# Batch 3 by quadrant attention, with copies and exponentials dealt anew, in a dilated attention and squared-ReLU FFN kernel

## The chip, the cores and the metric

The kernel runs on one core of one Trainium2 chip. The metric is the device time of an execution in microseconds, of which the median of several executions is given. Beside it stands one execution that the hardware profiler recorded; its span runs from the first to the last instruction.

Engines are named as the profile names them: PE (TensorE, matrix products; PEld its weight loads), DVE (VectorE), ACT (ScalarE), POOL (GpSimd, which here issues loads), SP (SyncE, which here issues stores and transposes).

## The reference

Eight batches of eight heads, 576 tokens, head dimension 64. Heads 0 to 3 attend to the last 32 tokens, heads 4 to 7 to every fourth of the last 128. The output of attention, 4608 tokens of 512, goes through a feed-forward net (FFN) with a squared ReLU.

```python
def _attn_ref(q, k, v):                      # (8, 8, 576, 64)
    window, dilation = 32, 4
    scores = 1.0 / np.sqrt(D) * np.matmul(q, k.transpose(0, 1, 3, 2))
    rel = pos[:, None] - pos[None, :]
    mask_plain = (rel >= 0) & (rel < window)
    mask_dil = (rel >= 0) & (rel < window * dilation) & (rel % dilation == 0)
    # heads 0-3 plain, heads 4-7 dilated; softmax over the unmasked scores
    return np.matmul(attn, v)

def _moe_ref(x, w_in, w_out):                # (4608, 512), (512, 2048), (2048, 512)
    h = np.maximum(x @ w_in, 0.0)
    return h * h @ w_out
```

## The kernel before

**FFN.** Tokens go through the FFN in tiles of 512, the first 1024 in tiles of 256. A tile is cut into groups, numbered over the whole kernel: groups 0 to 31 are the first 512 tokens, 32 to 63 the second, and from 64 on each tile of 512 has 32 groups. Of these the first 16 make one unit each of the first product (four matmuls of 512 columns over the four row blocks of `xT`, line 880), which ACT takes from PSUM with a ReLU (893) and DVE squares in place (894) into `h2T`. The last 16 are the second product (922): four token blocks `m`, each in four parts, and part `x` reads units 4x to 4x + 3. ACT copies each finished block to `osb` (928) and SP stores it. PSUM has four buffers `pf` for all this.

In a tile that is `early` (the first two of 512 that begin at token 512 or 1024) the first four units are begun on three row blocks of `xT` (order 0, 2, 1, 3) in two groups of six matmuls and closed with the fourth in two groups of two. A row block of `xT` is one pair of heads, `e` = 0 to 3.

**Attention** is woven into the groups. Pairs of heads come in the order e = 0, 2, 1, 3; e = 0, 1 are plain heads, 2, 3 dilated. There are two forms of it.

Batches 1 to 3 go through `step`. `kbd` and `vbd` hold block-diagonal matrices of two heads, so that matmuls are 128 x 128: `scores` (codes a, b) with an exponential on ACT and a mask multiplication on DVE, `pv` (codes o, p) with the weighted sum, the sum of weights, Ln and Exp on ACT (the reciprocal) and a multiplication into `xT`. Batch 2's dilated pairs and all of batch 3 take q and k from a transposing DMA (`cross`, into `xx`) and copy them into `qT` and `kbd` by `halves` (codes q, k), batch 1 transposes on PE. Batch 3 (`ADDED`) also adds overlapping pieces of the weights on DVE (`pm`), so that the sum of weights needs fewer matmul columns.

Batches 4 to 7 (`NATURAL`) go through `natural_step`. Their matmuls work on 64 x 64 quadrants of the array (line 529 in `quadrants`), four side by side, and v stays in rows (`load_v_rows`). Codes: K, Q, R are the copies of one batch into `k_both` (in `kbd`), `q_both` (in `qT`) and `last` (in `kbd`), all on DVE (499, 496, 504 and 507); each K code is two instructions, each Q code one, each R code two. S is the scores of a pair; B is the weighted sum of the pair before and then the scores of this pair, called a bundle here; E the exponential of one half of the scores and its mask (656, 658); L the four Ln (637, 638); X the Exp (642) and three multiplications into `xT` (645, 647). In the text L0 is the L of pair e = 0, E10 and E11 the two halves of pair 1.

**The order** is written out by hand. `PROGRAM` has a field for each group with the codes that follow it, and a list `steps` of group numbers and codes for the quadrant batches is merged behind it. Each engine takes its instructions in that order. For batch b the first bundle stands at group 32(b - 1) - 4, the others 8 groups apart, E at 2 and 3 groups after the bundle, L with the next bundle and X one group after. The copies stand in pairs of codes at 12, 10, 8, 6 and 3 groups ahead of the first bundle, the second code of each one group later. A tile needs all the batches that it overlaps: tile 96 to 127 (tokens 1536 to 2047) needs all of batch 3, tile 128 to 159 batch 4.

Buffers that decide about waits: `kbd` and `qT` are single, so copies for a batch wait until the batch before has read them; `xx` and `vbd` are double by batch; scores have two `pa` buffers, both used by every bundle; `po` and `pd` are single.

Of the kernel before, what the change touches and what calls it, by code (L numbers as in the profile page):

```python
# [12 lines left out]
RES = 4  # L13

ORDER = (0, 2, 1, 3)
# [13 lines left out]
    "| 2k0 1V2 | 1b2 1p0 | 1b1 1V3 1K3 | | 1p2 1p1f | 2a0 1b3 | 2k1l 2b0 2o0 1p3f 2k1h | 2q1 2k2 L3:x | | 2q2 2p0 "  # L29
    "L3:vwpdr 2a1 | | | 2b1 | 2o1 2a2 2v2 2q3 | | 2p1f | 2k3 | 2b2 2o2 | 2v3 | 2a3 2p2f L4:q10123 | 2b3 2o3 | 3k1 "  # L30
    "| 2p3 | 3q1v L4:q00123 | 3k0l | | 3a1 3k0h | | 3k2l | 3o1 3q0a | 3k2h | | | 3a0 | 3b1 | 3q2 | | 3p1 L4:x "
    "L4:V | 3v2 | 3b0 | 3a2 3q3l 3o0 3q3h 3k3 | | | 3o2 3b2 | | 3p0 3v3 | 3a3 | 3p2 | L5:q10123 3b3 | 3o3 | | | "
    "L5:q00123 3p3 L5:V | | | | | | | | | | | | L5:x | | | | L6:q00123 | | | | | | | | | | | | | L6:q10123"
)
# [27 lines left out]
def kernel(  # L62
# [9 lines left out]
    nc = tc.nc  # L72
    P = nc.NUM_PARTITIONS
    B, H, S, D = q.shape
# [3 lines left out]
    bf16 = mybir.dt.bfloat16  # L78
# [3 lines left out]
    ALU = mybir.AluOpType  # L82
# [12 lines left out]
    STAGE = (0, 1, 0, 2, 2, 2, 2, 2)  # L95
    ADDED = 3
    NATURAL = 4
    RING = 4 * S
# [5 lines left out]
    p_pool = ctx.enter_context(tc.tile_pool(name="p", bufs=4))  # L104
    pm_pool = ctx.enter_context(tc.tile_pool(name="pm", bufs=4))
    r_pool = ctx.enter_context(tc.tile_pool(name="r", bufs=2))
# [119 lines left out]
    def trans(b: int, e: int, nm: str, part: int, home: str):  # L226

        pool, name = (ps_f, "pf") if "f" in home else (ps_a, "pa")
        ps = pool.tile([P, 1024], bf16, name=name)
        t = staged(b, nm)  # L230
        copy = copier(nm, e, home, True)
        if b == 2:
            m0, n, pitch, cuts = 0, M, M, [(t[0:80, a, :, :], MS[a], 80) for a in range(2)]
        else:

            m0, n, pitch, cuts = MS[part], MN[part], 80, [(t[0:80, part, :, :], 0, 80)]
        pv_ = ps[:, 0 : 4 * pitch].rearrange("p (h c m) -> p h c m", h=2, c=2)
        for hl in range(2):
            for c in range(2):
                for src, c0, w in cuts:  # L240
                    nc.tensor.transpose(  # L241
                        pv_[:, hl, c, c0 : c0 + w], src[:, 2 * e + hl, P * c : P * c + P], ident[0:w, 0:w]
                    )
        ready[b, e, nm] = pv_[:, :, :, 0:n], m0, n, copy
        halves(e, nm, *ready[b, e, nm], (0,) if "l" in home else (0, 1))

    ready = {}

    def copier(nm: str, e: int, home: str, early: bool):
        act = "a" in home or "v" not in home and nm == "q" and e < NE // 2 and early  # L250
        return nc.scalar.copy if act else nc.vector.tensor_copy
# [31 lines left out]
    def blocks(b: int, e: int, part: int):  # L283
# [3 lines left out]
        if e < NE // 2:  # L287
            if b >= ADDED:
                return [(i, None, 16 * i, min(16 * i + 24, M)) for i in (range(4, NB) if part else range(4))]
            if part == 0:  # L290
                return [(i, None, 16 * i, min(16 * i + 24, 64)) for i in range(4)]
            return [(3, None, 64, 72)] + [(i, None, 16 * i, min(16 * i + 24, M)) for i in range(4, NB)]
# [7 lines left out]
    def half_at(b: int, e: int):  # L300

        if e < NE // 2:
            return (384, mask_p[:, 384:832]) if b >= ADDED else (352, mask_p)
        return (256, mask_d) if b in PARTED else (416, mask_h)

    pts, pms = {}, {}

    def scores(b: int, e: int, part: int):
# [5 lines left out]
        for i, r, m0, m1 in blocks(b, e, part):  # L314
# [14 lines left out]
            out=pt[:, off : off + n], in0=pt[:, off : off + n],  # L329
            in1=mask[:, off : off + n] if b < ADDED and mask is not mask_h else mask[:, 0:n], op=ALU.mult,  # L330
        )
        if b < ADDED:
            return
        pm = pms[e, part] = pm_pool.tile([P, 160], bf16, name="pm")

        def add(to, x, y):
            nc.vector.tensor_tensor(out=to, in0=x, in1=y, op=ALU.add)

        if e >= NE // 2:
            main = pt[:, off : off + 352].rearrange("p (r c) -> p r c", r=2)  # L340
            add(pm[:, 0:64].rearrange("p (r m) -> p r m", r=2), main[:, :, 64:96], main[:, :, 96:128])
            return
        i0, n = (3, 4) if part else (0, 3)
        v = pt[:, 96 * i0 : 96 * (i0 + n + 1)].rearrange("p (i r m) -> p i r m", r=RES, m=24)
        add(
            pm[:, 0 : 32 * n].rearrange("p (i r m) -> p i r m", r=RES, m=8),
            v[:, 0:n, :, 16:24], v[:, 1 : n + 1, :, 0:8],
        )
        if part:
            add(  # L350
                pm[:, 128:160].rearrange("p (r m) -> p r m", r=RES), v[:, n, :, 16:24],
                pt[:, 768:832].rearrange("p (r m) -> p r m", r=RES)[:, :, 0:8],
            )

    def pv(b: int, e: int, part: int, spare=None, name=""):
# [11 lines left out]
        if byr:  # L367
# [8 lines left out]
            mms.append((o3[:, :, 128:M], 8, rem))  # L376
            if b >= ADDED:
                pm = pms[e, part][:, 0:64].rearrange("p (r m) -> p r m", r=2)
                dms += [(d3[:, :, 0:64], main[:, :, 0:64]), (d3[:, :, 64:96], pm), (d3[:, :, 96:M], main[:, :, 128:176])]
            else:  # L380
                dms += [(d3[:, :, 0:96], main[:, :, 0:96]), (d3[:, :, 64:M], main[:, :, 96:176])]
            dms.append((d3[:, :, 128:M], rem))
        else:
            n = RES * MN[part]
            o3 = o[:, 0:n].rearrange("p (r m) -> p r m", r=RES)
            d3 = d[:, 0:n].rearrange("p (r m) -> p r m", r=RES)
            if not dil and b >= ADDED:

                i0 = 4 * part
                p4 = pt[:, 96 * i0 : 96 * i0 + 384].rearrange("p (i r m) -> p r i m", r=RES, m=24)  # L390
                d4 = d3.rearrange("p r (i m) -> p r i m", m=16)
                pm = pms[e, part]
                if part == 0:
                    dms.append((d4[:, :, 1:4, 8:16], p4[:, :, 1:4, 8:16]))
                    dms.append((d4[:, :, 1:4, 0:8], pm[:, 0:96].rearrange("p (i r m) -> p r i m", r=RES, m=8)))
                    dms.append((d4[:, :, 0, :], p4[:, :, 0, 0:16]))
                else:
                    dms.append((d4[:, :, 0:4, 8:16], p4[:, :, :, 8:16]))
                    b3 = pt[:, 288:384].rearrange("p (r m) -> p r m", r=RES)
                    b8 = pt[:, 768:832].rearrange("p (r m) -> p r m", r=RES)  # L400
                    dms.append((d4[:, :, :, 0:8], pm[:, 0:160].rearrange("p (i r m) -> p r i m", r=RES, m=8)))
                    dms.append((d4[:, :, 4, 8:16], b8[:, :, 8:16]))
                    mms.append((o3[:, :, 0:8], 3, b3[:, :, 16:24]))
                    mms.append((o3[:, :, 64:80], 8, b8))
                for i in range(4):
                    m1 = min(16 * i + 24, 64) if part == 0 else 16 * i + 24
                    mms.append((o3[:, :, 16 * i : m1], i0 + i, p4[:, :, i, 0 : m1 - 16 * i]))
            elif dil and part == 0:
                dms.append((d[:, 0:n], pt[:, 0:n]))
# [36 lines left out]
    def step(b: int, code: str):  # L446
# [6 lines left out]
        if what in "qk" and (b > XB or b == XB and e >= NE // 2):  # L453
            t = (qx if what == "q" else kx)[b % 2]
            halves(e, what, t[:, 2 * e : 2 * e + 2, :, :], 0, M, copier(what, e, home, b < ADDED), his)
        elif what in "qQkK" and "h" in home:
# [395 lines left out]
    def ffn_groups(tk0: int, nt: int):  # L852

        early = NT <= tk0 <= 2 * NT
        h2 = h2_pool.tile([P, NF, NT], bf16, name="h2T")
# [197 lines left out]
    groups[NF:G] = [head[y] for y in (8, 9, 12, 13, 10, 11, 14, 15)] + head[24:32]  # L1055
    COPIES = ("K00 K01", "K10 K11", "Q00 Q01", "Q10 Q11", "R00 R01")
    START = {NATURAL: (-10, -9, -3, -2, -1)}
    for b in range(NATURAL, B):
        base = G * (b - 1) - 4
        for y, codes in zip(START.get(b, (-12, -10, -8, -6, -3)), COPIES):  # L1060
            steps += [(base + y + x, b, code) for x, code in enumerate(codes.split())]
        for x, e in enumerate(ORDER):
            at = base + 8 * x
            steps.append((at, b, f"{'S' if b == NATURAL and x == 0 else 'B'}{e}"))
            steps += [(at + 2, b, f"E{e}0"), (at + 3, b, f"E{e}1"), (at + 8, b, f"L{e}"), (at + 9, b, f"X{e}")]
    steps.append((G * (B - 1) - 4, B - 1, f"P{ORDER[-1]}"))
    steps.sort(key=lambda x: (x[0], x[2][0] in "LX"))
    program = [x.split() for x in PROGRAM.split("|")]
    for code in program[0]:
        run(code)  # L1070
    for g, group in enumerate(groups):
# [10 lines left out]
        while steps and steps[0][0] <= g:  # L1082
            natural_step(*steps.pop(0)[1:])

# [29 lines left out]
```

## Time and profile before

| | us |
|---|---|
| median of 3 executions | 311.77 (309.77, 311.77, 312.34) |
| profiled execution | 308.71 |
| its span | 306.8 |
| PE busy | 295.2 (96%) |
| ACT busy | 203.4 (66%) |
| DVE busy | 177.7 (58%) |
| POOL busy | 96.1 (31%) |
| groups 64 to 95 on PE, start to start | 87.83 to 123.39 |
| groups 96 to 127 | 123.39 to 154.42 |
| groups 128 to 159 | 154.42 to 185.66 |
| groups 160 to 191 | 185.66 to 216.90 |

The busy times are shares of the whole span; stages differ much in them. The last four rows are read from the timeline of PE, from the first matmul of a tile's first product to that of the next tile. The granted clock of TensorE is 1.00 in every stretch.

### The profile page before, as it was taken

The page shows a single profiled execution, that of the slowest core. Times are in us where ns is not written, and L with a number is a line of the kernel's source. Part 1 is how long each engine was busy: PE and PEld are TensorE (multiplying, and loading weights), DVE is VectorE, ACT ScalarE, POOL GpSimd, SP SyncE. Part 2 cuts the span into 40 slices and gives each one's busy share as a digit, 9 for nine tenths or more (in the row PEclk, how much of TensorE's full clock was granted, in tenths as well). Part 3 has the DMA queues.
Part 4 walks back from the last instruction along what each step waited for, and adds up shares of the span by engine and source line. Part 5 has one row for each costly group of instructions (what it writes and reads, how often), then busy time and mean ns, then how long its engine had stood idle before and what let it go on. Part 6 is the DMA issues. An engine that isn't in the chain of part 4 may idle for free.

```text
span 306.8 us, 7297 instructions
## 1 busy us (share of the span) xinstructions
PE 295.2 (96%) x2870; PEld 172.3 (56%) x2903; DVE 177.7 (58%) x517; ACT 203.4 (66%) x439; POOL 96.1 (31%) x138
## 2 busy tenths in 40 slices
PE   8899999999999978999999999999999999999995
PEld 3599658769655544554455445544554445445543
DVE  1675567988988995468456855676563234104400
ACT  6888478869869744786579657865786576226511
POOL 8599683893065056230161208000000000000000
PEclk9999999999999999999999999999999999999999
DMA  8999999999979969998299869902200210121022
GB/s 115 196 180 214 204 162 224 174 150 185 154 111 196 157 100 204 139 148 131 69 133 152 103 142 103 164 16 65 61 2 13 68 61 0 35 71 34 0 64 75
DMA packets 80290, 35.09 MB, mean 114 GB/s; under 512 B 49920, under 2 KB 75648, under 8 KB 80256
## 3 DMA queue, kind: packets, MB, share of 16 engines
q0 software_dynamic: 46592, 18.23, 52.6%
q1 hardware_dynamic: 32976, 16.06, 26.0%
q8 instruction: 23, 0.38, 0.5%
q10 hardware_dynamic: 688, 0.33, 0.5%
q14 instruction: 11, 0.09, 0.1%
HBM read 36.90 MB, written 9.44 MB: 151 GB/s over the span
## 4 chain that ended last, share of the span: by engine, by line
PE 86%; DVE 6%; ACT 4%; issue 2%; ACTq 0%
PE pf L922 37%; PE pf L880 36%; PE po L674 2%; PE pa L529 2%; ACT h2T L893 2%; PE pd L529 1%; PE pa L241 1%; DVE h2T L894 1%; PE po L529 1%; PE po L427 1%; PE pa L704 1%; PE pd L429 1%; DVE kbd L499 1%; PE pf L756 1%; PE pa L323 1%
## 5 line engine op out<-in xcount | busy, mean ns | idle before, releaser
L880 PE MATMUL pf<-xT,w_in 128*128 128x512 bf16 (+1 forms) x693 | 130.4, 340 | 0.8
L922 PE MATMUL pf<-w_out_sb,h2T 128*128 128x512 bf16 (+2 forms) x570 | 128.6, 373 | 2.1 <-issue 1.4
L880 PEld LDWEIGHTS <-w_in 128*128 128x128 bf16 x704 | 76.9, 114 | 44.6 <-issue 1.1
L893 ACT ACTIVATE h2T<-pf 128x512 bf16<-128x512 f32 x144 | 82.4, 605 | 17.5 <-PE pf L880 17.0
L894 DVE TENSOR_TENSOR h2T<-h2T 128x512 bf16<-128x512 bf16 x144 | 60.1, 425 | 57.3 <-ACT h2T L893 53.0
L922 PEld LDWEIGHTS <-h2T 128*128 128x128 bf16 x592 | 54.7, 98 | 58.6
L928 ACT COPY osb<-pf 128x512 f32<-128x512 f32 (+1 forms) x36 | 20.7, 576 | 40.5 <-PE pf L922 37.6
L166 POOL DMA_DIRECT2D qb<-in_q_dram x18 | 13.6, 757 | 44.0 <-DMA xx<-qb 32.4
L645 DVE TENSOR_TENSOR xT<-po,rec 128x512 bf16<-128x512 f32 x16 | 11.1, 692 | 23.3 <-ACT rec L642 22.1
L656 ACT ACTIVATE pt<-pa 128x448 bf16<-128x448 f32 (+3 forms) x32 | 16.3, 509 | 9.3 <-DVE xT L647 9.3
L475 POOL DMA_DIRECT2D vd<-in_v_dram x16 | 9.9, 634 | 28.3 <-PE pa L529 24.8
L638 ACT ACTIVATE rec<-pd 64x512 f32<-64x512 f32 x32 | 18.6, 580 | 0.0
L183 POOL DMA_DIRECT2D vbd<-in_v_dram x20 | 13.9, 708 | 8.3 <-DMA kb<-in_k_dram 2.3
L327 ACT ACTIVATE pt<-pa 128x352 bf16<-128x352 f32 (+6 forms) x24 | 11.9, 506 | 4.1 <-PE pa L317 2.9
L431 ACT ACTIVATE rec<-pd 128x256 f32<-128x256 f32 (+2 forms) x19 | 7.8, 410 | 10.1 <-PE pd L429 10.1
L166 POOL DMA_DIRECT2D kb<-in_k_dram x18 | 13.6, 758 | 0.8 <-DMA vbd<-in_v_dram 0.4
L637 ACT ACTIVATE rec<-pa 64x64 f32<-64x64 f32 x32 | 7.0, 219 | 10.1 <-PE pa L529 9.5
L499 DVE COPY kbd<-xx 64x320 bf16<-64x320 bf16 (+1 forms) x32 | 13.0, 508 | 0.4
L484 POOL DMA_DIRECT2D vbd<-in_v_dram x16 | 12.5, 798 | 0.4 <-DMA qb<-in_q_dram 0.4
L442 DVE TENSOR_TENSOR xT<-po,rec 128x256 bf16<-128x256 f32 (+2 forms) x19 | 8.6, 454 | 6.5 <-ACT rec L432 5.7
L432 ACT ACTIVATE rec<-rec 128x256 f32<-128x256 f32 (+2 forms) x24 | 10.6, 443 | 0.8
L642 ACT ACTIVATE rec<-rec 128x576 f32<-128x576 f32 x16 | 10.9, 680 | 0.3
(128 smaller groups left out, 308.2 us busy)
## 6 DMA issues: line engine op xcount, KB each, us to landing
qb<-in_q_dram POOLq DMA_DIRECT2D x7, 320.0 KB, 5.4
kb<-in_k_dram POOLq DMA_DIRECT2D x7, 320.0 KB, 7.0
vd<-in_v_dram POOLq DMA_DIRECT2D x32, 64.0 KB, 6.2
w_in<-in_moe_w_in_dram POOLq DMA_DIRECT2D x4, 512.0 KB, 7.1
w_out_sb<-in_moe_w_out_dram POOLq DMA_DIRECT2D x4, 512.0 KB, 12.8
out_dram<-osb SPq DMA_DIRECT2D x16, 128.0 KB, 4.1
qb<-in_q_dram POOLq DMA_DIRECT2D x7, 256.0 KB, 7.2
kb<-in_k_dram POOLq DMA_DIRECT2D x7, 256.0 KB, 8.2
```

What stands on the lines that cost most here:

```text
L166: nc.gpsimd.dma_start(t[0:n, part, hs, :], src[b, hs, t0 : t0 + RES * n, :].rearrange("h (p r) d -> p h (r d)", r=RES))
L183: nc.gpsimd.dma_start(dst[rows, e, i0:i1, rows], v[b, 2 * e + hl, 64 * i0 : 64 * i1, :].rearrange("(i p) d -> p i d", p=64),)
L484: nc.gpsimd.dma_start(v_rows[b % 2][rows, e, :, :], v[b, 2 * e + hl, :, :].rearrange("(i p) d -> p i d", p=64))
L499: nc.vector.tensor_copy(k_both[rows, :, :].rearrange("p h (i m c j) -> p j c h i m", c=2, j=2, m=16)[:, jj, c, :, g::2, :], kx[b % 2][src, ...
L529: nc.tensor.matmul(out[sides[c]], lhs, rhs, start=begin, stop=True, skip_group_check=True)
L638: nc.scalar.activation(rec[to, 0:512], d[at, :], ACT.Ln)
L656: nc.scalar.activation(pt, sp[b, e][g][:, 0:n], ACT.Exp, scale=SCALE)
L880: nc.tensor.matmul(to, w_in_sb[piece][:, kt, c0 : c0 + 509 : 4], rhs, start=(kt == kts[0] and x == 0), stop=(kt == kts[-1] and x == per - ...
L893: nc.scalar.activation(hv, acc[u][:, :].rearrange("p (x n) -> p x n", x=per), ACT.Relu)
L894: nc.vector.tensor_tensor(out=hv, in0=hv, in1=hv, op=ALU.mult)
L922: nc.tensor.matmul(cur[m][:, c0:c1], h2[:, f, P * m : P * m + P], w_out_sb[:, f, c0:c1], start=(f == 0), stop=(f == NF - 1),)
L928: (nc.vector.tensor_copy if last and part == 1 else nc.scalar.copy)(osb[:, c0:c1], cur[m][:, c0:c1])
```

## The change

Batch 3 moves from `step` to `natural_step` (`NATURAL` is 3), with its v loaded in rows (`L3:V`). `ADDED`, `pm` and what they need are gone. The steps of batch 3 and of batch 4 get group numbers of their own; from batch 5 on the bundles stay where they were. Both exponentials E of a pair follow each other without a group between them: two groups behind their bundle, or one if the next bundle is no more than six groups on. The ten codes of the copies are dealt one to a group, from batch 5 on at 15, 14, 13, 12, 11, 10, 9, 7, 6 and 5 groups ahead of the first bundle; so K00, K01 and K10 stand behind groups 13, 14 and 15 of a tile, where all were behind group 16 or later. The tile that begins at token 1536 (groups 96 to 127) becomes `early` too. Within one group E and X come first, then copies, then a bundle, then L.

```diff
-    "L3:vwpdr 2a1 | | | 2b1 | 2o1 2a2 2v2 2q3 | | 2p1f | 2k3 | 2b2 2o2 | 2v3 | 2a3 2p2f L4:q10123 | 2b3 2o3 | 3k1 "
-    "| 2p3 | 3q1v L4:q00123 | 3k0l | | 3a1 3k0h | | 3k2l | 3o1 3q0a | 3k2h | | | 3a0 | 3b1 | 3q2 | | 3p1 L4:x "
-    "L4:V | 3v2 | 3b0 | 3a2 3q3l 3o0 3q3h 3k3 | | | 3o2 3b2 | | 3p0 3v3 | 3a3 | 3p2 | L5:q10123 3b3 | 3o3 | | | "
...
+    "L3:V 2a1 | | | 2b1 | 2o1 2a2 2v2 2q3 | | 2p1f | 2k3 | 2b2 2o2 | 2v3 | 2a3 2p2f L4:q10123 | 2b3 2o3 | | 2p3 | "
+    "L4:q00123 | | | | | | | | | | | | | | L4:x L4:V | | | | | | | | | | | L5:q10123 | | | | L5:q00123 L5:V | | | "
...
-    ADDED = 3
-    NATURAL = 4
+    NATURAL = 3
...
-        early = NT <= tk0 <= 2 * NT
+        early = NT <= tk0 <= 3 * NT
...
-    COPIES = ("K00 K01", "K10 K11", "Q00 Q01", "Q10 Q11", "R00 R01")
-    START = {NATURAL: (-10, -9, -3, -2, -1)}
+    BUNDLES = {3: (70, 76, 82, 87), 4: (92, 99, 107, 115)}
+    COPIES = {3: (62, 63, 64, 65, 66, 66, 67, 67, 68, 69), 4: (83, 84, 85, 86, 87, 88, 88, 89, 90, 91)}
     for b in range(NATURAL, B):
-        base = G * (b - 1) - 4
-        for y, codes in zip(START.get(b, (-12, -10, -8, -6, -3)), COPIES):
-            steps += [(base + y + x, b, code) for x, code in enumerate(codes.split())]
-        for x, e in enumerate(ORDER):
-            at = base + 8 * x
-            steps.append((at, b, f"{'S' if b == NATURAL and x == 0 else 'B'}{e}"))
-            steps += [(at + 2, b, f"E{e}0"), (at + 3, b, f"E{e}1"), (at + 8, b, f"L{e}"), (at + 9, b, f"X{e}")]
-    steps.append((G * (B - 1) - 4, B - 1, f"P{ORDER[-1]}"))
-    steps.sort(key=lambda x: (x[0], x[2][0] in "LX"))
+        ats = BUNDLES.get(b, tuple(G * (b - 1) - 4 + 8 * x for x in range(NE)))
+        for y, code in zip(
+            COPIES.get(b, [ats[0] - z for z in (15, 14, 13, 12, 11, 10, 9, 7, 6, 5)]),
+            ("K00", "K01", "K10", "K11", "Q00", "Q01", "Q10", "Q11", "R00", "R01"),
+        ):
+            steps.append((y, 1, b, code))
+        after = BUNDLES.get(b + 1, (G * b - 4,))[0]
+        for x, (e, at, to) in enumerate(zip(ORDER, ats, ats[1:] + (after,))):
+            steps.append((at, 2, b, f"{'B' if x or b > NATURAL else 'S'}{e}"))
+            y = at + 1 + (to - at > 6)
+            steps += [(y, 0, b, f"E{e}0"), (y, 0, b, f"E{e}1"), (to, 3, b, f"L{e}"), (to + 1, 0, b, f"X{e}")]
+        if b == B - 1:
+            steps.append((after, 2, b, f"P{ORDER[-1]}"))
+    steps.sort(key=lambda x: x[:2])
```

## The prediction

> **What bounds the kernel now.** I read the busy shares of the page, then stretches of the span, then the order of instructions on each engine around the places that change. The first view says that TensorE (PE) is the bound; the stretches say where it isn't.
>
> ```profile
> span 306.8 us, 7297 instructions
> PE 295.2 (96%) x2870; PEld 172.3 (56%) x2903; DVE 177.7 (58%) x517; ACT 203.4 (66%) x439; POOL 96.1 (31%) x138
> ```
>
> ```profile
> 88.00:98.00 10.00, 9.95 (x59) 5.49 (x59) 8.76 (x27) 8.07 (x19) 6.74 (x11) 1.00 1.33 172
> 98.00:112.00 14.00, 12.13 (x94) 6.66 (x93) 13.41 (x50) 9.05 (x20) 3.93 (x6) 1.00 1.02 128
> 112.00:123.60 11.60, 10.18 (x98) 5.70 (x100) 7.74 (x24) 5.89 (x14) 7.68 (x11) 1.00 1.34 183
> ...
> 186.00:201.50 15.50, 15.35 (x169) 8.32 (x169) 8.73 (x24) 13.64 (x29) 4.69 (x7) 1.00 1.17 129
> ```
>
> After the length of a stretch come PE, PEld, DVE, ACT and POOL busy, then the granted clock (1.00 throughout). 88.0 to 123.6 holds groups 64 to 95, in which batch 3's attention runs: DVE (VectorE) works 29.9 of 35.6 us there and PE stands still for 3.3. At 186 the steady state of batches 5 to 7 has PE full and DVE half empty. So the change works where DVE is the limit, and I followed DVE's queue.
>
> ```profile
> 112.20 0.39 PE L427 MATMUL po<-pt,vbd 128*128 128x32 bf16 x6 [1.97 <-DVE xT L442]
> ...
> 120.16 0.36 PE L529 MATMUL pa<-qT,kbd 64*64 64x96 bf16 x16 [0.79 <-DVE qT L496]
> ...
> 201.40 4.48 PE L922 MATMUL pf<-w_out_sb,h2T 128*128 128x512 bf16 x20
> ```
>
> ```profile
> 202.25 0.47 DVE L647 TENSOR_TENSOR xT<-pa,rec 64x64 bf16<-64x64 f32 x2
> 202.75 0.43 DVE L894 TENSOR_TENSOR h2T<-h2T 128x512 bf16<-128x512 bf16 x1
> 203.09 0.39 DVE L658 TENSOR_TENSOR pt<-pt,mask_p 128x448 bf16<-128x448 bf16 x1
> 203.56 0.43 DVE L894 TENSOR_TENSOR h2T<-h2T 128x512 bf16<-128x512 bf16 x1
> 203.94 0.36 DVE L658 TENSOR_TENSOR pt<-pt,mask_p 128x384 bf16<-128x384 bf16 x1
> 204.21 3.30 DVE L499 COPY kbd<-xx 64x320 bf16<-64x320 bf16 x8
> 207.54 0.94 DVE L496 COPY qT<-xx 64x1152 bf16<-64x1152 bf16 x2
> ```
>
> Each line gives start, length, engine, line of code and operation, and in brackets the idle time before it. The first two are PE's waits on DVE in the stage. The rest is one tile of the steady state: the two L894 are the squares of units 14 and 15; only then come the eight K copies (L499). PE starts the second product at 201.40, and its 16th matmul, at 201.48 + 15 x 0.2165 = 204.73, reads unit 15. That square is done at 203.99: 0.74 us in hand.
>
> **Prices.** FFN matmul 0.2165 us (16 from 87.83 to 91.29), a group of four 0.866, 32 groups 27.71. DVE, start to start: square 0.34, K pair 0.90 (g=0) and 0.77 (g=1) from the 3.30 us of eight, Q copy 0.47, R pair 0.43, the three multiplies of an X 1.11, masks 0.36 and 0.28. ACT: relu 0.51, the four Ln of an L 1.42, Exp of an X 0.6, the two score exponentials 0.43 and 0.42, an output copy 0.47. An E's exponentials begin 0.85 after DVE's X multiply begins, since they wait for its tails (L647). Bundles on PE, from the end of one FFN run to the next: 0.70 (190.27 to 190.97), otherwise 0.78; scores alone 0.30.
>
> **Removed, groups 64 to 95.** The time before is 35.56 us (87.83 to 123.39): 27.71 of FFN; 14 insertions of batch 3's attention, 0.20+0.27+0.17+0.20+0.37+0.20+0.45+0.49+0.38+0.18+0.34+0.15+0.34+0.33 = 4.07; the wait before 112.20, 2.13; batch 4's first scores with their wait, 1.69. Also gone are the pm additions, batch 3's v spreads, and its 16 q copies and 24 k copies, about 12 us of DVE and ACT work (0.24 a q copy, 0.47, 0.23 and 0.19 a k copy); that work is priced through the waits it caused. Loads: ten v DMAs by POOL become ten others of the same bytes, before the same need: nothing.
>
> **Added, same groups.** S0 0.30 and bundles 0.70 + 3 x 0.78 give 3.34, so without waits 31.05. Waits, by following the queues from 87.23 us, where DVE comes free for batch 3's copies in both kernels:
> - K00 87.23 to 88.13; batch 2's last xT can't start before 89.10 (its Exp ends 89.05); K01, K10, K11 to 91.92; two squares, Q00, Q01 to 93.54; two squares, Q10, Q11 to 95.16. PE is through group 70 at 94.1 (0.2 of that waiting for u0's relu). S0 waits 1.1 and ends at 95.5.
> - B2 behind group 76 goes at 100.8 unhindered. L0, a relu, X0, E2, masks done at 106.35; B1 behind group 82 goes at 106.7: no wait, 0.3 in hand.
> - Five groups on, L2 (from 107.5), an output copy, X2, E1, masks end at 112.25, while PE is at 111.8. B3 waits 0.5 and ends at 113.1.
> - From 112.25 DVE is never idle: four K pairs 3.34, Q00, X1, the masks of e3 (pv of B0 possible at 118.2), three Q copies to 119.5. PE reaches B0 at 117.4; its scores need the last Q: 1.8 late.
> Waits 0.2+1.1+0.5+1.8 = 3.6, stage 34.65: **a gain of 0.9 us** where 4.5 was to be had. Bounds: 4.5 gained if every wait goes, 1.0 lost if the last Q copy comes 1.9 later still. I take 0.8.
>
> As to the multiplication in quadrants, the rows say 4.07 us before against 0.70 + 3 x 0.78 = 3.04 after. The Trainium skill, "TensorEngine Tiling (Array Packing)", section "Theoretical Speedup", allows four 64x64 tiles up to a fourfold gain; that would make 1.0 us of the 4.07 and the stage 2.0 us better than I have it. The same page under "PSUM Bottleneck" warns that tiling doesn't speed up the evacuation behind it, which speaks against the change, and DVE's 13.41 busy of 14.00 us sides with the warning.
>
> **Groups 96 to 127.** Beginning this tile on three row blocks costs the same matmuls. It moves the need for xT's fourth block from the fourth matmul of the tile to the 13th, 2.0 us later; X3 is then ready 3 us ahead. The price comes on ACT: four relus fall due at once, then L0, and PE, which has four pf buffers, waits at group 106 for the relu of 102, 0.45. B1 comes one group earlier (107), and DVE gets K00, K01 between the squares 109 to 111: square 111 done at 142.2 against 141.7 wanted, 0.55 late. Sum **1.0 lost**, bounds 0 and 2; I take 1.1, since each restart costs about 0.05 (112.15 to 112.20).
>
> **Groups 128 to 159 and 160 to 191.** This part makes the forecast. K00 now stands at place 13 of 32, K01 at 14, K10 at 15, where before all stood from 16 on. After X2, from 202.75: K00 to 203.65, square 14 to 203.99, masks E10 and E11 (now together) to 204.62, K01 to 205.52, square 15 done at 205.95. PE wants it at 204.73: late by 1.28 with 0.06 of signalling. In the tile before (X2 done 171.40, K copies 3.40 us) the same sum gives 1.25. What cover there was, 0.74 us, is used up. Nothing gives it back, as PE is the bound; behind the wait B3, L1 and X1 only move along, and the Q copies are through before X1 needs DVE. **1.3 lost, twice**; bounds 0 (if PE comes that late anyway) and 2.1 (K10 too ahead of the square). The tile after 191 has no copies: exponentials together push square 15 by 0.36 inside its 0.74, nothing. The transposes: the k part lands some 5.6 after issue at 192.87, at 198.5, ahead of 202.75; no wait.
>
> **Sum:** -0.8 + 1.1 + 1.3 + 1.3 = +2.9. The profiled execution took 308.71 (span 306.8, 1.9 around it), so 311.6 for such an execution. The median shown is 311.77, 1% above the profiled one; I predict for the median, 311.77 + 2.9 = 314.7.
>
> **Rivals.**
> (B) Stage 64 to 95 reaches the steady pace, 31.05 + 0.5: -4.0, while the squares are late as above: 311.77 - 4.0 + 3.7 = 311.5. For it: DVE has some 4 us free between the masks of E0 (98.3) and X0 (104.2). Against: batch 4's K copies can't use that, kbd being read by B1's scores until 107.5.
> (C) Faster: DVE's queue never decides. One mechanism, the price of a K copy: at the 0.23 of the L272 row a pair takes 0.46. Then S0's wait of 1.1 goes, B0's shrinks by the 1.5 that four pairs save, and square 15 comes 0.9 earlier, which leaves 0.4 a tile: -0.9 - 1.1 - 1.5 + 0.5 + 2 x 0.4 = -2.2. At 0.25 a pair the squares are in time and B0's wait is gone: -0.9 - 1.1 - 1.8 + 0.4 = -3.4, 308.4. It is faster than before from about 0.6 us a pair downwards. Against: L499 is the same instruction on the same data, 0.51 mean of 32. C stands also for any other way in which DVE comes through sooner.
> (D) Batch 4's transposes hold its Q copies. They are chained by POOL's loads (issued from 87.06) and the last had landed at 109.8, when POOL's next load into their source starts (109.80 L166); DVE wants it at 115.5. Should it land at 118 instead, B0 shifts by 2.5: 317.3. Against: that chain is not touched, and 5.7 us lie between.
> (E) The change does nothing: excluded, 4 us of matmuls are replaced and copies move in three tiles.
>
> **How the numbers follow.** Forecast 0.62, its own range 313.0 to 316.8; B 0.08, C 0.15, D 0.15. The runs before spread from 309.77 to 312.34, so about 1%, 3.1 us, is what a measurement tells from no change. My sum lies just under that line with more that can add (waits that I put at zero, 0.3 in hand at B1) than subtract: of the forecast's 0.62, 0.37 is over 1% and 0.25 within. With D slower is 0.52. Within: 0.25 and 0.03 of B, 0.28. Faster: C and 0.05 of B, 0.20. For the range I leave out most of C below and the end of D above: 309.0 to 318.0.
>
> **What would show it.** Right: in the two tiles after 155 us the L922 run shows a gap of over 1 us ahead of its 16th matmul, released by DVE h2T; DVE's order there has L499 between the L894; the stage of groups 64 to 95 still has waits of 1 us before the first L529 and nearly 2 before the one at its end. Wrong: tiles at 155 and 186 of 31.0 us as now, or a stage under 33.5 us. A wait of PE on DVE qT at B0 of over 3 us would speak for D.

## The result, and the profile after

The change makes the kernel slower. Over 15 executions each, the median is 313.25 us after (311.89 to 314.32) and 310.74 us before (309.08 to 312.34); the ratio is 1.0081, 95% interval 1.0058 to 1.0105. The profiled execution took 313.71 us.

The head of the page of after, span and busy times:

```profile
span 311.6 us, 7465 instructions
PE 295.3 (95%) x2977; PEld 170.6 (55%) x3011; DVE 172.7 (55%) x487; ACT 203.7 (65%) x439; POOL 95.9 (31%) x138
```

PE and ACT are busy as long as before, DVE 5 us less, and the span is longer: the time went into waits. The stretches of after (length, then busy PE, PEld, DVE, ACT, POOL, clock, DMA share, GB/s), which begin 1.5 us earlier in the program than the same numbers did before, because the head of this execution was that much longer:

```profile
88.00:98.00 10.00, 8.45 (x61) 4.41 (x60) 8.42 (x22) 5.39 (x11) 7.97 (x11) 1.00 1.30 170
98.00:112.00 14.00, 13.74 (x162) 7.30 (x163) 7.45 (x21) 10.75 (x24) 3.82 (x6) 1.00 1.03 113
112.00:123.60 11.60, 9.84 (x142) 4.94 (x142) 9.31 (x26) 6.57 (x16) 3.04 (x6) 1.00 1.02 173
...
157.14:189.60 32.46, 31.00 (x338) 15.83 (x340) 19.08 (x53) 22.34 (x48) 8.86 (x14) 1.00 0.83 122
```

DVE is full no longer in the middle of the stage (7.45 of 14.00), but still is busy for 8.42 of the first 10.00 us, where PE now stands still for 1.55, and for 9.31 of 11.60 near the end, where PE stands for 1.76. And the steady tile, in which PE was full, now has 1.46 us of idle PE in 32.46. PE's timeline shows where (start, length, engine, line, operation, idle time before it and what ended it; line 477 was 529, 828 was 880, 870 was 922, 841 was 893, 842 was 894):

```profile
97.34 0.36 PE L477 MATMUL pa<-qT,kbd 64*64 64x96 bf16 x16 [1.46 <-DVE qT L444]
...
121.99 0.36 PE L477 MATMUL pa<-qT,kbd 64*64 64x96 bf16 x16 [0.74 <-DVE qT L444]
...
134.92 1.89 PE L828 MATMUL pf<-xT,w_in 128*128 128x512 bf16 x8 [0.38 <-ACT h2T L841]
...
177.33 1.25 PE L870 MATMUL pf<-w_out_sb,h2T 128*128 128x512 bf16 x5 [1.05 <-DVE h2T L842]
...
209.68 1.25 PE L870 MATMUL pf<-w_out_sb,h2T 128*128 128x512 bf16 x5 [0.94 <-DVE h2T L842]
```

These are batch 3's first scores, batch 4's first scores, group 106 on a relu, and the 16th matmul of the second product in the two tiles after 157 us. DVE's queue ahead of the fourth of them:

```profile
174.12 0.88 DVE L447 COPY kbd<-xx 64x320 bf16<-64x320 bf16 x2
174.80 0.43 DVE L842 TENSOR_TENSOR h2T<-h2T 128x512 bf16<-128x512 bf16 x1
175.16 0.64 DVE L606 TENSOR_TENSOR pt<-pt,mask_p 128x448 bf16<-128x448 bf16 x2
175.82 0.99 DVE L447 COPY kbd<-xx 64x320 bf16<-64x320 bf16 x2
176.85 0.43 DVE L842 TENSOR_TENSOR h2T<-h2T 128x512 bf16<-128x512 bf16 x1
```

The K copies (447, formerly 499) stand on either side of square 14, both ahead of square 15, which ends at 177.28. PE waits until 177.33.

The main view of this study is the length of the four tiles on PE, from the start of a tile's first product to that of the next, in each kernel's profiled execution. What follows group 192 takes the same time before and after, within 0.3 us (89.9 and 89.7 us to the end of the span). The ratios are those on record; they leave out three executions that took over 1.5% longer than their kernel's fastest, and differ by up to 0.003 from the quotients of the medians named in the text.

| kernel | 64 to 95 | 96 to 127 | 128 to 159 | 160 to 191 | sum against before | ratio of times, 95% interval |
|---|---|---|---|---|---|---|
| before | 35.56 | 31.03 | 31.24 | 31.24 | 129.07 | 1 |
| after | 35.57 | 32.26 | 32.46 | 32.35 | +3.57 | 1.0081 (1.0058 to 1.0105) |
| copies_late | 35.46 | 31.61 | 31.23 | 31.24 | +0.47 | 0.9989 (0.9960 to 1.0019) |
| before_copies | 35.55 | 31.84 | 32.04 | 32.03 | +2.39 | 1.0067 (1.0034 to 1.0101) |
| copies_first | 35.33 | 33.88 | 34.24 | 34.06 | +8.44 | 1.0241 (1.0190 to 1.0291) |
| exps_apart | 35.45 | 31.88 | 32.07 | 32.06 | +2.39 | 1.0057 (1.0023 to 1.0092) |
| batch3_alone | 35.40 | 31.19 | 31.24 | 31.23 | -0.01 | 0.9971 (0.9941 to 1.0002) |
| scores_later | 36.20 | 32.22 | 32.56 | 32.34 | +4.25 | 1.0057 (1.0024 to 1.0089) |
| scores_again | 33.90 | 32.26 | 32.39 | 32.34 | +1.82 | one execution, 310.76 us |
| k4_ahead | 33.93 | 32.28 | 32.38 | 32.33 | +1.85 | 1.0012 (0.9983 to 1.0041) |
| not_early | 35.34 | 31.85 | 32.38 | 32.37 | +2.87 | 1.0094 (1.0061 to 1.0127) |
| pool_probe | 35.45 | 32.29 | 32.34 | 32.34 | +3.35 | one execution, 312.30 us |
| all_mended | 32.84 | 31.23 | 31.23 | 31.23 | -2.54 | 0.9839 (0.9793 to 0.9885) |
| mended_later | 32.32 | 31.81 | 31.23 | 31.24 | -2.47 | 0.9898 (0.9869 to 0.9927) |

### The profile page after: what moved, and what is told of

Same layout as the page of the kernel before. It is cut to its first block, busy times and chain, and to the rows that moved or that the text cites. A ratio compares the mean times of both kernels' runs of the same rounds, so it can differ in the third digit from the quotient of the medians.

```text
span 311.6 us, 7465 instructions
## 1 busy us (share of the span) xinstructions
PE 295.3 (95%) x2977; PEld 170.6 (55%) x3011; DVE 172.7 (55%) x487; ACT 203.7 (65%) x439; POOL 95.9 (31%) x138
## 4 chain that ended last, share of the span: by engine, by line
PE 73%; DVE 9%; ACT 8%; DMA 5%; issue 3%; POOL 1%; DVEq 0%; ACTq 0%; POOLq 0%
PE pf L828 32%; PE pf L870 32%; DVE kbd L447 4%; DMA w_in<-in_moe_w_in_dram 3%; DMA kb<-in_k_dram 2%; PE pa L477 2%; ACT rec L586 2%; ACT h2T L841 2%; DVE qT L444 1%; PE pd L477 1%; DVE h2T L842 1%; ACT rec L590 1%; DVE xT L593 1%; PE pa L238 1%; PE po L477 1%
## 5 line engine op out<-in xcount | busy, mean ns | idle before, releaser
L593 DVE TENSOR_TENSOR xT<-po,rec 128x512 bf16<-128x512 f32 x20 | 13.8, 692 | 34.0 <-ACT rec L590 32.6
L604 ACT ACTIVATE pt<-pa 128x448 bf16<-128x448 f32 (+3 forms) x40 | 18.0, 501 | 13.6 <-DVE xT L595 13.6
L423 POOL DMA_DIRECT2D vd<-in_v_dram x20 | 12.7, 649 | 36.7 <-PE pa L477 32.7
L586 ACT ACTIVATE rec<-pd 64x512 f32<-64x512 f32 x40 | 23.2, 579 | 0.0
L447 DVE COPY kbd<-xx 64x320 bf16<-64x320 bf16 (+1 forms) x40 | 16.2, 507 | 0.5
L477 PEld LDWEIGHTS <-mk 64*64 64x64 bf16 x240 | 8.8, 106 | 9.2 <-issue 7.1
L590 ACT ACTIVATE rec<-rec 128x576 f32<-128x576 f32 x20 | 13.6, 680 | 0.3
L477 PE MATMUL pd<-pt,mk 64*64 64x192 bf16 (+4 forms) x140 | 10.0, 252 | 0.7 <-DVE pt L606 0.5
L322 ACT ACTIVATE pt<-pa 128x352 bf16<-128x352 f32 (+4 forms) x16 | 7.8, 500 | 3.1 <-PE pa L312 1.9
L444 DVE COPY qT<-xx 64x1152 bf16<-64x1152 bf16 x20 | 9.5, 475 | 0.5
```

Of the source, the lines that this page charges most:

```text
L447: nc.vector.tensor_copy(k_both[rows, :, :].rearrange("p h (i m c j) -> p j c h i m", c=2, j=2, m=16)[:, jj, c, :, g::2, :], kx[b % 2][src, ...
L477: nc.tensor.matmul(out[sides[c]], lhs, rhs, start=begin, stop=True, skip_group_check=True)
L586: nc.scalar.activation(rec[to, 0:512], d[at, :], ACT.Ln)
L590: nc.scalar.activation(rec[:, :], rec[:, :], ACT.Exp, scale=-1.0)
L593: nc.vector.tensor_tensor(out=tok[:, :, 0:128], in0=byr(o[:, :]), in1=byr(rec[:, 0:512]), op=ALU.mult)
L604: nc.scalar.activation(pt, sp[b, e][g][:, 0:n], ACT.Exp, scale=SCALE)
```

## The experiments

All are edits of after, save before_copies, which is an edit of before.

**The place of the copies.** copies_late keeps the whole change but deals the copies of batches 5 to 7 so that all K copies stand behind square 15 again.

```diff
-            COPIES.get(b, [ats[0] - z for z in (15, 14, 13, 12, 11, 10, 9, 7, 6, 5)]),
+            COPIES.get(b, [ats[0] - z for z in (12, 11, 10, 9, 8, 7, 6, 5, 3, 2)]),
```

> The changed kernel with one part undone: from batch 5 on the copies stand 12 to 5 and 3, 2 groups ahead of the first bundle again, so no K copy stands among the squares of a tile's first product. Theory (K copies ahead of square 15 in DVE's queue hold PE at the 16th matmul of the second product): the waits of 0.47, 1.05 and 0.94 us that PE has there in groups 96 to 191 go, the three tiles take 31.8, 31.2 and 31.2 us, and the time falls by 2.5 to that of the kernel before: ratio 1.000. Rival one (the exponentials together jam ACT) and rival two (the tile begun on three row blocks): the ratio stays at 1.008 and the tiles at 32.3 to 32.5.

Measured: 309.89 us against 310.11. DVE's timeline in the tile of groups 128 to 159:

```profile
172.12 0.43 DVE L842 TENSOR_TENSOR h2T<-h2T 128x512 bf16<-128x512 bf16 x1
172.47 0.72 DVE L606 TENSOR_TENSOR pt<-pt,mask_p 128x448 bf16<-128x448 bf16 x2
173.32 0.43 DVE L842 TENSOR_TENSOR h2T<-h2T 128x512 bf16<-128x512 bf16 x1
173.66 3.31 DVE L447 COPY kbd<-xx 64x320 bf16<-64x320 bf16 x8
```

The same eight copies, now in one run behind the second square; PE's view of waits has no line on `h2T` any more, and the two tiles are back at 31.23 and 31.24. Moving the copies takes away 3.10 of the 3.57 us that after lost. It takes the whole of these two tiles' loss with it, so in them the exponentials together cost something only where the copies have used up the cover. Groups 96 to 127 keep 0.58 of their loss: the wait on a relu at group 106 is still there.

before_copies is the other direction: the kernel before, with nothing changed but the copies of batches 5 to 7, dealt as in after.

```diff
-        for y, codes in zip(START.get(b, (-12, -10, -8, -6, -3)), COPIES):
-            steps += [(base + y + x, b, code) for x, code in enumerate(codes.split())]
+        if b == NATURAL:
+            at = [y + x for y in START[b] for x in range(2)]
+        else:
+            at = (-15, -14, -13, -12, -11, -10, -9, -7, -6, -5)
+        steps += [(base + y, b, code) for y, code in zip(at, " ".join(COPIES).split())]
```

> The kernel before with one part done: from batch 5 on the copies are dealt singly, 15 to 9 and 7 to 5 groups ahead of the first bundle; exponentials stay apart, batch 3 stays with block-diagonal matrices. Theory: in the tiles of groups 96, 128 and 160 square 15 comes behind K00 and K01, 1.8 us of copies, of which 0.74 are covered; with some signalling PE waits 0.9 to 1.0 a tile, together +2.9, ratio 1.009, stage 64 to 95 unchanged at 35.6. Rivals (exponentials, early tile): ratio 1.000.

Measured: 0.80 us more in each of the two steady tiles and 0.81 in groups 96 to 127, and a ratio whose interval lies wholly above 1. That is the price of the copies alone, without any other part of the change, and a little less than the 0.9 to 1.0 a tile that had been expected.

copies_first puts all four K codes ahead of the square.

```diff
-            COPIES.get(b, [ats[0] - z for z in (15, 14, 13, 12, 11, 10, 9, 7, 6, 5)]),
+            COPIES.get(b, [ats[0] - z for z in (15, 15, 15, 15, 11, 10, 9, 7, 6, 5)]),
```

> The changed kernel with the suspected cost doubled: from batch 5 on all four K pairs stand at the place of the first. Theory: squares 14 and 15 come behind four pairs in place of two, 1.5 to 1.6 us more in each of the three tiles, tiles of 33.9 to 34.1 us, +4.7 against the changed kernel, ratio to the kernel before 1.023. Rivals: as the changed kernel, 1.008.

Measured: 318.48 us. The steady tiles are 1.71 to 1.78 us longer than in after. PE's timeline in one of them:

```profile
179.54 0.39 PE L870 MATMUL pf<-w_out_sb,h2T 128*128 128x512 bf16 x1 [2.14 <-DVE h2T L842]
180.44 1.25 PE L870 MATMUL pf<-w_out_sb,h2T 128*128 128x512 bf16 x5 [0.52 <-DVE h2T L842]
```

Now square 14 is late as well and PE waits twice. The two pairs added ahead of the squares, K10 and K11, take 1.50 us where they stand in one run (after, 177.31), so they cost about what they take. The price follows the number of pairs ahead of the square.

**The exponentials.** exps_apart gives the second exponential of a pair a group of its own again.

```diff
-            steps += [(y, 0, b, f"E{e}0"), (y, 0, b, f"E{e}1"), (to, 3, b, f"L{e}"), (to + 1, 0, b, f"X{e}")]
+            steps += [(y, 0, b, f"E{e}0"), (y + (to - at > 6), 0, b, f"E{e}1"), (to, 3, b, f"L{e}"), (to + 1, 0, b, f"X{e}")]
```

> The changed kernel with one part undone: the two exponentials of a pair stand a group apart again wherever bundles are more than six groups apart. Theory: the mask of the second half (0.28 to 0.3 us) leaves the place ahead of square 15, so the three waits shrink by 0.3 each, ratio 1.005; the wait at group 106 (0.38) may go too, since the relu of group 102 comes ahead of the second exponential: 1.004. Rival one (exponentials are the whole cause): ratio 1.000. Rival two: 1.008.

Measured: each of the three tiles is 0.29 to 0.39 us shorter than in after, the same lengths as before_copies within 0.04. So the loss of a steady tile divides into 0.80 for K00 and K01 and 0.3 to 0.4 for the mask of E11, which comes ahead of square 15 when the two exponentials stand together. In groups 96 to 127 the gain is another one: the wait for the square is as in after, and of the delay at group 106 (0.54 us in after) 0.19 is left.

**Batch 3 alone.** batch3_alone has the copies late, the exponentials apart and the fourth tile begun on four row blocks; the quadrant attention of batch 3 and its group numbers are all that is left of the change.

```diff
-        early = NT <= tk0 <= 3 * NT
+        early = NT <= tk0 <= 2 * NT
```

(and the edits of copies_late and exps_apart)

> Of the change only batch 3 by quadrants is left, with the own group numbers of batches 3 and 4; from batch 5 on the copies stand where they were, exponentials are apart where bundles are more than six groups apart, and tile 96 to 127 isn't begun on three row blocks. Theory (in stage 64 to 95 the saved waits come back at S0, B3 and B0, because DVE's queue is full): stage 35.5 as in both kernels, the tiles behind it 31.1 to 31.3, ratio 1.000. Rival (the quadrants save their 4.5 us and the other parts eat it): stage near 31.5, ratio 0.988.

Measured: 309.66 us against 310.28, and four tiles of the same length as before in sum, 0.01 apart. The part that replaces 4.07 us of matmuls with 3.4 (the prediction has 3.04) brings nothing by itself.

**Where that gain went.** The stage of groups 64 to 95 has two large waits in after, at batch 3's first scores (S0) and at batch 4's (in B0). scores_later moves the first of them two groups back.

```diff
-    BUNDLES = {3: (70, 76, 82, 87), 4: (92, 99, 107, 115)}
+    BUNDLES = {3: (72, 76, 82, 87), 4: (92, 99, 107, 115)}
```

> The changed kernel with one size changed: batch 3's first scores S0 behind group 72 in place of 70; nothing else moves. Theory (S0 stands 1.7 us waiting for Q copies that are done 8.0 us into the stage, and B1, from which DVE's later chain counts, comes earlier by as much): that wait goes, stage 33.8 to 34.1, ratio 1.003. Rival (the time is given back at B0, since DVE's work sets the end of the stage): the wait at B0 grows from 2.0 to 3.6, stage 35.5, ratio 1.008.

Measured: the wait at S0 shrank to some 0.4 us, but the stage was longer, 36.20. For 3.41 us from 120.11 on the granted clock was 0.50, which lengthened the stage by 1.46 us; and in this execution the first K copy waited 0.72 us for the transposing DMA, and batch 4's eight K copies took 3.61 us instead of 3.33. The timed ratio, 1.0057, is 0.0024 below that of after, which is within their intervals. This run left the size open, so the same kernel was profiled a second time, as scores_again.

> The kernel scores_later looked at once more. Its profile had 1.5 us at the end of the stage at a granted clock of 0.66. If that comes from the waits that stand there now, it comes again and the stage is 36.2; if it was chance, the stage is 34.7 (S0's wait shrunk from 1.75 to 0.45, K copies 0.3 longer).

Measured: the clock was 1.00 throughout, the stage 33.90, 1.67 us shorter than in after. PE's timeline at S0, with no wait in brackets:

```profile
88.13 8.14 PE L828 MATMUL pf<-xT,w_in 128*128 128x512 bf16 x36
96.20 0.39 PE L477 MATMUL pa<-qT,kbd 64*64 64x96 bf16 x18
```

The wait at S0 was 1.7 us of the stage, and nothing behind it took its place: the waits at B3 and B0 are as long as in after, 0.4 and 1.8 us. The rest of the difference to scores_later, 0.84 us, lies at S0 and B0, where the copies of that execution came later.

k4_ahead leaves S0 and moves batch 4's copies up, three K codes ahead of the multiplication X2 in DVE's queue.

```diff
-    COPIES = {..., 4: (83, 84, 85, 86, 87, 88, 88, 89, 90, 91)}
+    COPIES = {..., 4: (83, 83, 83, 84, 84, 85, 85, 86, 90, 91)}
...
-            steps.append((y, 1, b, code))
+            steps.append((y, -1 if y == 83 else 1, b, code))
```

> The changed kernel with only DVE's order of batch 4's copies changed: K00, K01, K10 directly behind B1 and ahead of X2's multiplications, where DVE is idle for 2.9 us, and the rest one or two groups earlier. Theory (order in DVE's queue, not the amount of its work): the copies are done before X2's Exp is, the waits of 0.4 at B3 stays and that of 2.0 at B0 goes, stage 33.5 to 33.7, ratio 1.002. Rival (batch 4's transposes land too late for earlier copies, or DVE's work itself is the bound): stage 35.5 or longer, ratio 1.008.

Measured: stage 33.93, 1.64 us shorter than in after. DVE's timeline in after, where it waited ahead of X2, and in k4_ahead:

```profile
112.46 0.69 DVE L593 TENSOR_TENSOR xT<-po,rec 128x512 bf16<-128x512 f32 x1 [2.87 <-ACT rec L590]
```

```profile
109.19 2.74 DVE L447 COPY kbd<-xx 64x320 bf16<-64x320 bf16 x6 [0.23 <-PE pa L477]
111.94 0.69 DVE L593 TENSOR_TENSOR xT<-po,rec 128x512 bf16<-128x512 f32 x1
```

The copies begin as soon as B1's scores have read the old `kbd`, and fill time in which DVE would wait for X2's Exp. The Q copies are then through at 116.82 instead of 121.94 (in an execution whose head was 0.7 us shorter), and PE's wait on them at B0 is gone. With this single edit the timed ratio is 1.0012, its interval on both sides of 1; by the tiles the kernel is still at +1.85, the stage 1.63 us shorter than before and the three tiles behind it, where the squares are late, 3.48 longer.

**The fourth tile.** not_early takes back only the beginning on three row blocks (the edit shown for batch3_alone).

> The changed kernel with one part undone: the tile of groups 96 to 127 isn't begun on three row blocks. Theory: the wait of 0.38 at group 106 for a relu goes, and a small one comes at the tile's fourth matmul, wanted at 125.5 where the fourth row block is done at 125.6: 0.1 to 0.2. Tile 32.0 to 32.1 in place of 32.26, the other tiles unchanged, ratio 1.007 against 1.008, not to be told apart by the time. Rival (the early tile is the cause of the loss): ratio 1.000. Rival (it is what lets the stage end early): ratio 1.012 or more.

Measured: groups 96 to 127 take 31.85 instead of 32.26, 0.41 us less, a little more than expected; the ratio, 1.0094, isn't told from that of after. In the trace of all_mended, which begins the tile on three row blocks too, the wait on the relu doesn't appear, and exps_apart has little of it: the early beginning costs it mainly together with exponentials that stand together in ACT's queue.

**Loads beside copies.** In the stage, copies that run while POOL issues loads last longer than elsewhere (see the last section). pool_probe adds eight needless loads of v to after, issued by POOL beside the K and Q copies of groups 160 to 191, to see whether this lengthens the wait there.

```diff
+        if g == 173:
+            probe = mask_d[:, 0:512].rearrange("p (x i d) -> p x i d", x=4, d=D)
+            nc.vector.memset(probe[:, :, :, 0:1], 0.0)
+            for x in range(4):
+                for hl, rows in enumerate(sides):
+                    nc.gpsimd.dma_start(
+                        probe[rows, x, :, :], v[7, 2 * x + hl, 0:128, :].rearrange("(i p) d -> p i d", p=64)
+                    )
```

> The changed kernel with eight needless loads issued by POOL into an unused mask buffer, released by a small DVE memset behind group 173, so that POOL issues while DVE does the K and Q copies of batch 7, where it had nothing to issue. Theory (DVE's copies and POOL's issuing of loads lengthen each other, which is why S0's wait was 1.75 and not 1.1): K pairs of 1.0 to 1.3 in place of 0.88, Q copies 0.55 to 0.7 in place of 0.47, the wait of PE in that tile 1.2 to 1.8 in place of 0.94, the tile before it unchanged. Rival (the Q copies waited for something else): 0.88, 0.47 and 0.94 to 1.0.

Measured, POOL's and DVE's timelines:

```profile
204.49 6.00 POOL L1040 DMA_DIRECT2D mask_d<-in_v_dram  x8 [11.29 <-ACT rec L590]
```

```profile
205.16 0.88 DVE L447 COPY kbd<-xx 64x320 bf16<-64x320 bf16 x2
...
206.87 0.86 DVE L447 COPY kbd<-xx 64x320 bf16<-64x320 bf16 x2
...
209.81 1.45 DVE L444 COPY qT<-xx 64x1152 bf16<-64x1152 bf16 x3
```

The pairs take 0.88 and 0.86 us, where after had 0.88 and 0.87 in the same place without loads, and the wait at the 16th matmul was 0.93 against 0.94. These loads did not lengthen the K copies beside them, and of the Q copies one took 0.48 instead of 0.45. That any load that POOL issues does so is refuted. It was the loads that waited: two of the eight, beside the K pairs, took 1.06 and 1.12 us where the shortest took 0.60.

**All mended.** all_mended puts together what the runs had shown: copies late, exponentials apart, S0 two groups later, batch 4's K copies ahead of X2, and the other bundles of batches 3 and 4 up to one group later.

```diff
-    BUNDLES = {3: (70, 76, 82, 87), 4: (92, 99, 107, 115)}
+    BUNDLES = {3: (72, 76, 82, 88), 4: (93, 100, 108, 116)}
...
-    COPIES = {..., 4: (83, 84, 85, 86, 87, 88, 88, 89, 90, 91)}
+    COPIES = {..., 4: (83, 83, 83, 84, 84, 85, 85, 86, 91, 92)}
```

(with the edits of copies_late, exps_apart and k4_ahead; the last loads of batch 5 are issued one group later)

> A version meant to beat both: batch 3 by quadrants and the early tile stay; S0 behind group 72, B3 behind 88, batch 4's bundles behind 93, 100, 108, 116, batch 4's K00, K01, K10 directly behind B1; from batch 5 on copies as before; exponentials apart where bundles are more than six groups apart. Theory: stage 31.05 of work and 0.5 of waits, 31.6; tile 96 to 127 31.2, as the relu of group 102 is no more behind both exponentials; the next two 31.24; 3.8 us less than the kernel before, ratio 0.988. Rival (DVE's amount of work is the bound in the stage): 34 or more there, ratio 0.995 or above.

Measured: 305.87 us against 310.28, faster than the kernel before, and by the two ratios than after, with which it wasn't timed side by side. Its stretches by tile, and the one row of PE's waits that lies in the four tiles (total, times, longest):

```profile
88.32:121.16 32.84, 32.38 (x362) 16.32 (x361) 25.02 (x66) 22.51 (x50) 14.99 (x21) 1.00 1.12 155
121.16:152.39 31.23, 31.19 (x342) 15.94 (x341) 19.74 (x53) 22.64 (x49) 10.82 (x16) 1.00 1.10 153
```

```profile
PE pd L477 <- DVE pt L606: 0.2, 1, 0.2
```

PE is busy for 31.19 of 31.23 us in a steady tile and 32.38 of 32.84 in the stage. The stage is 2.72 us shorter than before, so the quadrants' gain comes out once most of what stood ahead of PE's operands in DVE's queue has been moved. It isn't the 31.6 that was expected. The work alone takes 31.5 and not 31.05 (next section), and from one FFN matmul to the next PE still waits 1.3 us: 0.2 each for the first relu and at S0, 0.4 at B3 and 0.5 at B0, most of it inside bundles, where the views count PE as busy.

mended_later moves the last three bundles of batch 3 and the first two of batch 4 on by one group where all_mended still has small waits (`BUNDLES = {3: (72, 77, 83, 89), 4: (94, 101, 108, 116)}`, batch 4's copies one group later except the two Rs, batch 5's v again one group later).

> The version all_mended with the bundles of the stage moved on by a group: B2 behind 77, B1 83, B3 89, B0 94, then 101. In all_mended PE still waited 0.4 at B3 and 0.7 at B0 for exponentials and masks; the fourth row block of batch 3 is then wanted 3.5 us after B0 where Ln, Exp and multiplication take 3.2. Theory: those waits shrink by 0.87 and 0.4, stage 31.7 in place of 32.84, ratio 0.981. Rival (the latency behind a bundle only moves, and now the fourth row block or the first scores of batch 4 are late in the next tile): ratio 0.984 or above with a wait at the next tile's fourth row block.

Measured: 307.28 us against 310.96. The stage is 0.52 us shorter than in all_mended and the next tile 0.58 longer: work was moved over the boundary, as the rival had it, and new waits came, 0.43 at 108.0 on a square that stands behind X0 and the masks of pair 2 in DVE's queue, 0.28 at 124.3 on `xT`, and 0.16 at 125.5 on a relu. The four tiles take 126.60 and 126.53 us. That all_mended is truly the faster of the two isn't shown: they were timed in different comparisons and their intervals overlap.

## Why the prediction was right

The forecast was +2.9 us, to 314.7; the median is 313.25, which is +2.51 over the 310.74 of the kernel before (the 311.77 that the forecast was added to is the median of three of these executions). The four tiles of the two profiles give +3.57. So the sum was 0.7 short of what the tiles show, and the timed difference lies on the other side of it, perhaps because the kernel before ran more often at a lower clock (last section): that +2.51 comes so close to +2.9 is in part luck. Below, delays are counted from the start of one FFN matmul to the start of the next. The idle times in brackets are 0.16 us shorter, since they begin at the modelled end of the matmul before (0.38 us long, 0.22 apart). By its steps:

- **Groups 128 to 191: right in place, order and size.** Forecast 1.3 a tile; measured 1.22 and 1.11. The queue was as foretold, K00, square 14, two masks, K01, square 15, and the gap stands at the 16th matmul, which came 1.22 and 1.10 late (1.28). From the start of K00 to the end of square 15 DVE took 3.16 and 3.03 us where the sum had 3.20. Single prices were less exact: in the first of the two tiles K00 held DVE for 0.68 (174.12 to 174.80) and K01 for 1.03 (175.82 to 176.85), where 0.90 was put in for each. The reading of the slack was a little off too: from 201.40 the 16th matmul starts at 204.64, not 204.73, so 0.66 us were in hand in that tile; in the two tiles before it 0.76 and 0.77. before_copies and exps_apart show the two parts as separate prices, 0.80 and 0.3 to 0.4.
- **Groups 96 to 127: right.** Forecast 1.1, measured 1.23, with 0.54 at group 106 (0.45) and 0.64 at the square (0.55). not_early gives 0.41 for the first of these, net of a wait of 0.16 that comes at the fourth matmul instead.
- **Groups 64 to 95: the mechanism right, the size off.** Forecast a gain of 0.9, taken as 0.8; measured 0.0. No wait came at B2 and B1, as said; B3 waited 0.4 (0.5) and B0 1.8 (1.8), allowing for FFN matmuls that are missing from the records there (19 of 20 are recorded behind B1 and behind B3, 11 of 12 behind B0). Two terms were mis-sized. The wait at S0 was 1.7 where 1.1 was put in. The K copies ended where the sum had them, but the four Q copies behind them took 0.62, 0.59, 0.45 and 0.57 where the price list had 0.47 from start to start, 0.4 us more in all, and the squares between them a little more. POOL was issuing loads beside all four. The other term is the work itself: S0 and the four bundles were put in at 3.34 us, and without waits they take 0.41 (S0, scores_again) and 0.80, 0.87, 0.79 and 0.94 (B2, B1, B3, B0, mended_later), 3.81 in all. Their price had been read from the modelled end of a run of FFN matmuls, that of the part removed from start to start. So the stage without waits is 31.5 us and not 31.05, and the attention of a batch goes from 4.07 us to 3.4, a saving of 0.7 where the prediction has 1.0.
- **After 191, and the transposes: nothing**, as forecast.

Of the rivals, B (the stage at its steady pace) did not come, but scores_again and k4_ahead show that each of the two large waits it needed gone was one edit away, 1.67 and 1.64 us; with both edits and some more all_mended is at 32.84, still 1.3 above B's pace. The reason given against it was incomplete: batch 4's K copies can't use the time before B1, but they can use that between B1 and X2, where after's order left DVE idle. C wanted cheaper K copies; a pair took 0.88 to 0.99. D wanted late transposes; PE's wait at B0 was on DVE's Q copies, and it went when these were moved ahead. The fourfold gain that the prediction cites for the tiles did not come near, 4.07 against 3.4 us. Its warning about the evacuation behind a tiled multiplication isn't tested as such: what held PE at S0 and B0 were copies of operands, and batch3_alone shows only that the shorter matmuls gained nothing until DVE's order was changed.

## What to carry to other kernels

When work is dealt finely over the groups of a bound engine, look up what stands behind each new place in its own engine's queue: here two pairs of copies ahead of an operand that had some 0.7 us in hand cost the bound engine 0.8 us in every tile. A saving on the bound engine showed only once the queue that feeds it had little needless ahead of what was wanted next. So sum the queue up to each operand in order, and move the copies into the time in which that queue waits for a third engine.

## What the runs showed of the hardware

**Copies and loads lengthen each other, by who comes first.** In the fourteen traces there are 272 Q copies (64x1152 bf16, on DVE). The 203 with no load being issued by POOL beside them took 0.444 to 0.459 us, all of them. Of the 69 with an issue beside them 27 took over 0.47, up to 0.718, in the stage of all_mended. Its POOL and DVE timelines:

```profile
112.99 1.15 POOL L163 DMA_DIRECT2D qb<-in_q_dram  x1 [10.92 <-issue]
114.13 0.73 POOL L163 DMA_DIRECT2D kb<-in_k_dram  x1
```

```profile
113.85 2.66 DVE L444 COPY qT<-xx 64x1152 bf16<-64x1152 bf16 x4
```

Four copies took 2.66 us where four take 1.91 elsewhere (k4_ahead, 114.91), and an issue took 1.15 where most of this kind take some 0.7. The Trainium skill, "SBUF — State Buffer", section "SBUF: two separate sides", says that GpSimd and certain VectorE copies share a pair of ports as an exclusive lock, and that the loser waits for the whole instruction. The rows agree, and show who waits. The 27 long copies are those that began when an issue had been running for 0.25 us or more and had over 0.19 us left; each ended 0.25 to 0.29 us after that issue. The 17 copies that began in the first 0.22 us of an issue kept their time, and the issue ended 0.12 to 0.32 us after the copy. So an issue beside the copy isn't enough, as the other 42 show: it must be well under way when the copy begins. Where it had only just begun, the issue was the one that ended late. Three of the four Q copies ahead of S0 in after met that condition.

**The granted clock differs between executions.** Of the 65 executions of the kernel before in the three comparisons that list it, 31 have a mean granted clock of TensorE of at least 0.998 and 34 have less (0.986 to 0.997); in each comparison the medians of the latter are 1.1 to 2.1 us longer. Two of the traces are of such executions, before_copies and scores_later: each has one stretch of 3.41 us at 0.50, from 12.73 (before the first FFN tile) and from 120.11 (behind the longest break in that stage's FFN matmuls, 3.03 us). Half pace for 3.41 us costs up to 1.7 us, about the difference of the medians. Of the 40 executions of copies_late, batch3_alone, k4_ahead and exps_apart only 2 are below 0.998, but 4 of 10 are of scores_later and 5 of 10 of before_copies. Executions at 0.998 or more alone differ from the kernel before by +0.3, +0.1, +1.7 and +2.3 us for the first four, where the sums of the four tiles say +0.47, -0.01, +1.85 and +2.39; for all_mended it is -3.7 against -2.54. So part of what the timed ratios show is that the kernel before ran more often at a lower clock. This may also be why after was timed at +2.51 where its tiles say +3.57; the list of clocks is not there for that comparison, and why some kernels have more such executions than others stays open.
